# Weight conversion of the second MLP group spread over ten head slots instead of eight, its scale and split two slots later

## The chip, the core and the metric

One NeuronCore of a Trainium2 chip runs the whole program. The metric is the device time of one execution in microseconds (us); lower is better. Engine names are those of the profile: PE (matrix products), PEld (loading of PE's weights), DVE (vector), ACT (activation), POOL (GpSimd) and SP (its queue issues most loads and stores).

## What is computed

Eight batches of eight attention heads, with 576 positions of 64 numbers each, a mask by blocks of 64, softmax, and then an MLP over all 4608 tokens with d_model 512 and d_ff 2048. Cut to what matters:

```python
scores = where(block_i >= block_j, q @ k.T / 8, -1e9)          # per batch and head
attn   = softmax(scores) @ v                                    # (8, 8, 576, 64)
x      = attn.transpose(0, 2, 1, 3).reshape(4608, 512)
h      = x @ w_in                                               # (4608, 2048)
sp     = maximum(h, 0) + log1p(exp(-abs(h)))
out    = (h * erf(sp)) @ w_out                                  # (4608, 512)
```

The MLP weights arrive as 64-bit floats. The kernel splits every operand of the MLP into a high and a low 16-bit part, so that each product is three 16-bit matmuls.

## The kernel before, in words

**MLP tiling.** d_ff is cut into 16 blocks f of 128 columns, each with two halves s (w_in and w_out). The blocks form two groups: group 0 is f = 0 to 7, group 1 is f = 8 to 15. Tokens are cut into 18 tiles of 256. One piece of work is a tile with a group; it has four units of two blocks each. A unit (`moe_unit`, line 181) has 4 up steps of 6 matmuls each (line 193, h = w_in . x) followed by one gate (`gate`, line 152: ACT lines 161 to 164 and 168, DVE lines 165 to 167, POOL line 169), and 8 down steps with 12 matmuls together (line 202, o += gate . w_out). The last unit of a piece has two stores more, and in group 1 one step that loads what group 0 has stored. Group 0 of a tile stores partial sums to DRAM, group 1 adds them.

**Weights.** A half goes through three stages. `load_raw` (line 111) brings its 0.5 MB from DRAM by the SP queue (line 115, two buffers). `to_f32` (line 118, "conversion") makes 32-bit floats from the 64-bit ones: ACT lines 122 and 128, DVE lines 123, 124 and 125. When a whole group is converted, `scale_group` (line 565) finds its scale (`scale_w`, line 130: a DVE sum, a small matmul, some small DVE operations; then `scale_bg` for the batches known). Then `split_w` (line 143) makes the 16-bit parts of one block: two ACT instructions (line 148) and two DVE instructions (line 149).

**Order of the work.** The order is written out by hand in the loop over head slots n = 0 to 66. In slot n the program emits: the load of head n + 3 (lines 400 to 408), the row maxima of head n + 2 (PE line 432, DVE line 435), the probabilities of head n (PE lines 478 and 479, six pairs a slot, and ACT line 483), every second slot the product with v (line 527), and every fourth the normalisation of four heads, whose result goes to DRAM as x and is read back by `load_x` (line 225, SP queue) when a batch is complete. `merge` spreads the lists of steps evenly over the slot. The instructions go to the engines by this order as a priority: one whose inputs are there early can be placed ahead of its entry. Each engine and each queue then takes its own instructions in order.

Four tables place the rest. `TOF` says how many halves are converted in a slot, `SCALE_AT` in which slot a group's scale is made, `SPLIT` how many blocks are split in a slot. `RATE` says how often `moe1` (line 271) is called: 12 times a slot before slot 20, 28 times from slot 20 on. Each call emits one MLP step, if there is one. A unit is taken from the queue only when its blocks have been split:

```python
if jobs and len(done) >= 2 * jobs[0][2] + 2:      # in moe1: both blocks of the unit are split
    ...
if len(downs) > lag[-1] or not jobs and downs:    # the down part of an earlier unit beside it
    lists.append((downs.pop(0), 0, 1))
```

`next_job` (line 255) lets a tile into the queue when its batch is ready: tiles 0 and 1 from slot 10, tiles 2 and 3 from slot 18, tiles 4 and 5 from slot 26. Group 1 of a tile enters only after group 1 has been scaled. What the slots don't emit is emitted after slot 66 by a loop that calls `moe1` until nothing is left.

By the tables of before, group 1 is converted in slots 11 to 18 (two halves each), scaled in slot 20 and split in slots 20 to 23 (two blocks each). From slot 12 to the end of slot 66, 4 calls of `moe1` find nothing to emit; all 4 are in slot 23. After slot 66 there remain 117 up steps and 257 down steps.

Of the kernel before, what the change touches and what calls it, by code (L numbers as in the profile page):

```python
# [32 lines left out]
def tile_attention_moe(ctx: ExitStack, tc: tile.TileContext, qk, v, w, maskrows, selws, out):  # L33
# [264 lines left out]
    with tc.tile_pool(name="apool", bufs=2) as apool, tc.tile_pool(name="spool", bufs=1) as spool, \  # L298
# [266 lines left out]
        def scale_group(g):  # L565
            scale_w(g, bank)
            scaled[g] = True
            for b in known:
                scale_bg(b, g)
# [81 lines left out]
        def late(kind, steps):  # L651

            def run(f):
                tc.cur_priority += PRIO.get(kind, 0)
                f()
                tc.cur_priority -= PRIO.get(kind, 0)
            return [lambda f=f: run(f) for f in steps]
# [1 line left out]
        PRIO = {}  # L659
        WARM = 10  # L660
        LQ = 0.1
        TOF = {0: 1, 1: 1, 2: 2, 3: 2, 4: 2, 5: 2, 6: 2, 7: 2, 8: 2} | {n: 2 for n in range(11, 19)}
        SCALE_AT = {9: 0, 20: 1}
        SPLIT = {9: 2, 10: 3, 11: 3, 20: 2, 21: 2, 22: 2, 23: 2}
        def conv():
            fs = HALVES[len(conved)]
            conved.append(fs)
            if len(raws) < len(conved):
                next_raw()
            to_f32(*fs, raws[fs])  # L670
            if len(raws) == len(conved):
                next_raw()
# [11 lines left out]
        for n in range(N + 3):  # L684
# [38 lines left out]
            ready = ready_at.get(n, ready)  # L723
            for _ in range(TOF.get(n, 0)):
                lists.append((late("conv", [conv]), 0, 1))
            if n == 2:
                lists.append(([selects], 0.5, 0.6))
            if n in SCALE_AT:
                lists.append(([lambda n=n: scale_group(SCALE_AT[n])], 0, 0.1))
            if n in SPLIT:  # L730
                lists.append((late("conv", [split_next] * SPLIT[n]), 0.1, 1))
            if n < 2:
# [52 lines left out]
```

## Time and profile before

| what | value |
|---|---|
| median of 3 runs | 1236.84 us (1234.63 to 1239.13) |
| profiled execution | 1233.12 us, of which its span is 1231.3 us |
| mean granted PE clock | 0.968 of full |
| PE busy | 1149.8 us (93%) |
| DVE busy | 824.7 us (67%) |
| ACT busy | 863.3 us (70%) |
| POOL busy | 478.7 us (39%) |
| HBM | 118.15 MB read, 28.31 MB written |

The span runs from the first to the last instruction of the program. Busy shares are means over stages that differ: slots 0 to 9 are attention and weights alone, slots 11 to 66 have both attention and MLP, and the end is MLP alone. Matmuls are pipelined and their ends are modelled, so a busy PE is not yet a PE at its peak. A slot isn't marked in the trace; it is found by the six pairs of matmuls of line 478 that each head has.

### The profile page before, as it was taken

To read this page: it belongs to the slowest core of one execution; us is meant where nothing else is said; L and a number is where in the kernel's file an instruction comes from. 1 tells how busy PE (TensorE), PEld (TensorE's weight loads), DVE (VectorE), ACT (ScalarE), POOL (GpSimd) and SP (SyncE) were. 2 spreads that over 40 slices of the span, in tenths; PEclk is the share of its full clock that TensorE was granted. 3 is DMA by queue.
4 is the path that set the end of the run, shared out by engine and by line. 5 is a ranking of instruction groups with operands and counts; after the bars stand their busy time and mean duration, and the time that the engine had idled before them with its cause. 6 is when DMAs were issued, how large, how long until landed. Compare 5 with 4: busy or idle time off the path is not lost.

```text
span 1231.3 us, 23115 instructions
## 1 busy us (share of the span) xinstructions
PE 1149.8 (93%) x8874; PEld 796.0 (65%) x8874; DVE 824.7 (67%) x1559; ACT 863.3 (70%) x1675; POOL 478.7 (39%) x459
## 2 busy tenths in 40 slices
PE   6867899899999999999999999999989999999997
PEld 3545666566666667767666676776766766666663
DVE  5877887797577767677667666666667644455555
ACT  4665777577677776777777676777767776766664
POOL 7454545535444544445354444435444322100000
PEclk9876899989999999999999999999999999999999
DMA  8676667735545455453554455444544221221202
GB/s 231 171 211 161 166 186 219 179 91 122 120 133 138 110 129 124 129 136 102 124 137 95 114 125 121 115 124 116 120 114 108 57 67 57 72 69 52 65 23 85
DMA packets 94091, 148.19 MB, mean 120 GB/s; under 512 B 7610, under 2 KB 44794, under 8 KB 93982
## 3 DMA queue, kind: packets, MB, share of 16 engines
q1 hardware_dynamic: 69696, 93.34, 24.9%
q0 software_dynamic: 23616, 53.15, 20.3%
q8 instruction: 70, 1.15, 0.4%
q10 hardware_dynamic: 670, 0.23, 0.1%
q14 instruction: 39, 0.32, 0.1%
HBM read 118.15 MB, written 28.31 MB: 119 GB/s over the span
## 4 chain that ended last, share of the span: by engine, by line
PE 34%; DVE 26%; ACT 25%; DMA 7%; issue 6%; POOL 2%; ACTq 0%; DVEq 0%; SPq 0%; POOLq 0%
PE m_h L193 11%; PE o L202 10%; DVE m_r L165 6%; DVE m_r L166 5%; DVE m_r L167 5%; PE u L527 4%; ACT m_r L162 4%; ACT m_r L161 4%; ACT m_r L164 4%; ACT m_r L163 4%; ACT m_gh L168 3%; DVE mx L435 3%; PE s L432 2%; PE t L478 2%; DMA qk<-qk 2%
## 5 line engine op out<-in xcount | busy, mean ns | idle before, releaser
L193 PE MATMUL m_h<-xh,w 128*128 128x256 f16 x2304 | 473.7, 275 | 13.1 <-DVE m_r L167 12.1
L193 PEld LDWEIGHTS <-w 128*128 128x128 f16 x3456 | 327.3, 99 | 147.0 <-issue 18.1
L202 PE MATMUL o<-w,m_gh 128*128 128x512 f16 x1152 | 332.9, 382 | 4.7 <-ACT m_gh L168 3.8
L193 PE MATMUL m_h<-xl,w 128*128 128x256 f16 x1152 | 316.3, 275 | 0.0
L169 POOL TENSOR_TENSOR m_gl<-m_r,m_gh 128x512 f16<-128x512 f32 x114 | 136.1, 1193 | 267.7 <-ACT m_gh L168 234.7
L435 DVE TENSOR_REDUCE mx<-s 64x1 f32<-64x288 f32 (+4 forms) x384 | 173.9, 469 | 93.5 <-PE s L432 92.9
L165 DVE SCALAR_TENSOR_TENSOR m_r<-m_r,m_r 128x512 f32<-128x512 f32 x144 | 116.2, 807 | 166.4 <-ACT m_r L164 161.6
L168 ACT CAST m_gh<-m_r 128x512 f16<-128x512 f32 x144 | 88.9, 617 | 173.3 <-DVE m_r L167 171.5
L202 PE MATMUL o<-w,m_gl 128*128 128x512 f16 x576 | 203.7, 384 | 0.0
L483 ACT ACTIVATE p<-t 128x288 f32<-128x288 f32 (+4 forms) x384 | 143.8, 383 | 68.4 <-PE t L479 60.4
L478 PE MATMUL t<-qk 69*128 69x288 f32 (+4 forms) x384 | 167.8, 438 | 13.1 <-DVE mx L435 6.1
L432 PE MATMUL s<-qk 68*64 68x288 f32 (+3 forms) x384 | 148.5, 421 | 24.6 <-DMA qk<-qk 18.6
L408 POOL TENSOR_TENSOR qk<-st,qk 64x576 fp32r<-64x576 f32 x64 | 94.9, 1484 | 128.8 <-DMA qk<-qk 121.0
L161 ACT ACTIVATE m_r<-m_h,c,bs 128x512 f32<-128x512 f32 (+3 forms) x192 | 123.9, 665 | 28.9 <-PE m_h L193 27.4
L202 PEld LDWEIGHTS <-m_gh 128*128 128x128 f16 x1152 | 100.4, 98 | 60.9 <-issue 6.9
L495 DVE TENSOR_TENSOR p<-p,p 128x832 f16<-128x832 f32 x80 | 81.6, 1020 | 62.6 <-ACT p L494 62.5
L479 PE MATMUL t<-qk 128*128 128x288 f32 (+4 forms) x384 | 120.7, 316 | 0.0
L166 DVE SCALAR_TENSOR_TENSOR m_r<-m_r 128x512 f32<-128x512 f32 x144 | 116.7, 810 | 3.2
L405 POOL TENSOR_TENSOR qk<-st,qk 64x576 fp32r<-64x576 f32 x64 | 98.5, 1539 | 29.6 <-ACT qk L415 13.0
L163 ACT ACTIVATE m_r<-m_r,c 128x512 f32<-128x512 f32 x144 | 103.7, 720 | 2.7 <-ACT m_r L162 0.6
L164 ACT ACTIVATE m_r<-m_r,c 128x512 f32<-128x512 f32 x144 | 103.6, 719 | 2.2 <-ACT m_r L163 0.3
L162 ACT ACTIVATE m_r<-m_r,c 128x512 f32<-128x512 f32 x144 | 103.7, 720 | 2.0
(113 smaller groups left out, 1459.9 us busy)
## 6 DMA issues: line engine op xcount, KB each, us to landing
qk<-qk POOLq DMA_DIRECT2D x52, 432.0 KB, 4.7
st<-qk SPq DMA_DIRECT2D x64, 288.0 KB
qk<-qk POOLq DMA_DIRECT2D x64, 288.0 KB, 5.0
raw<-w SPq DMA_DIRECT2D x32, 512.0 KB
v<-v SPq DMA_DIRECT2D x16, 640.0 KB
x_d<-xs POOLq DMA_DIRECT2D x32, 288.0 KB, 3.3
xh<-x_d SPq DMA_DIRECT2D x36, 256.0 KB
xl<-x_d SPq DMA_DIRECT2D x36, 256.0 KB
```

The costliest lines, as they stand in the source:

```text
L161: nc.scalar.activation(r0s[:, :, lo:hi], h[:, :, lo:hi], AF.Tanh, bias=const(p1), scale=bss[b][g][:, 0:1])
L162: nc.scalar.activation(r1, r0, AF.Square, bias=const(b1), scale=a1)
L163: nc.scalar.activation(r0, r1, AF.Square, bias=const(b2), scale=a2)
L164: nc.scalar.activation(r0, r0, AF.Square, bias=const(b3), scale=a3)
L165: nc.vector.scalar_tensor_tensor(out=r0, in0=r0, scalar=c4, in1=r1, op0=ALU.add, op1=ALU.mult)
L166: nc.vector.scalar_tensor_tensor(out=r0, in0=r0, scalar=c5, in1=r0, op0=ALU.add, op1=ALU.mult)
L193: nc.tensor.matmul(h[:, k, :], lhsT=wf[:, a, sl], rhs=x[:, cc, :], start=cc == 0 and i == 0, stop=cc == NCC - 1 and i == 2)
L202: nc.tensor.matmul(o[c], lhsT=a[:, sl], rhs=wf[:, b_, :], start=u == u0 and k == 0 and not lo and b_ == 2, stop=u == u1 - 1 and k == nu - ...
L432: nc.tensor.matmul(dst[:r, :w_], lhsT=qh[:K, i * P : i * P + r], rhs=kh[:K, k0 : k0 + w_], start=True, stop=True)
L435: nc.vector.tensor_reduce(out=mx[:r, col : col + 1], in_=src, axis=AX.X, op=ALU.max, negate=True)
L478: nc.tensor.matmul(s[:kk, :w_], lhsT=kh[:K, ks], rhs=qh[:K, q0 : q0 + w_], start=True, stop=False)
L483: nc.scalar.activation(p32s[part][:kk, c : c + w_ - skip], s[:kk, skip:w_], AF.Exp, scale=SCALE)
```

## The change

It edits three of the tables. Group 1's halves are converted one a slot in slots 11 to 14 and two a slot in slots 15 to 20. Its scale goes from slot 20 to slot 22, and its blocks are split in slots 22 to 25 instead of 20 to 23, two a slot as before. Group 0's entries (slots 0 to 11) stay. No instruction is added or taken away.

```diff
-        TOF = {0: 1, 1: 1, 2: 2, 3: 2, 4: 2, 5: 2, 6: 2, 7: 2, 8: 2} | {n: 2 for n in range(11, 19)}
-        SCALE_AT = {9: 0, 20: 1}
-        SPLIT = {9: 2, 10: 3, 11: 3, 20: 2, 21: 2, 22: 2, 23: 2}
+        TOF = {0: 1, 1: 1, 2: 2, 3: 2, 4: 2, 5: 2, 6: 2, 7: 2, 8: 2} | {n: 1 for n in range(11, 15)} | {n: 2 for n in range(15, 21)}
+        SCALE_AT = {9: 0, 22: 1}
+        SPLIT = {9: 2, 10: 3, 11: 3, 22: 2, 23: 2, 24: 2, 25: 2}
```

## Rows read from the trace of the kernel before

**Rows 1.** The page, parts 1: span; busy time, share, instructions of each engine.
```profile
span 1231.3 us, 23115 instructions
PE 1149.8 (93%) x8874; PEld 796.0 (65%) x8874; DVE 824.7 (67%) x1559; ACT 863.3 (70%) x1675; POOL 478.7 (39%) x459
```

**Rows 2.** Windows, line 478 alone: stretch, its length, PE busy (instructions), PEld, clock, DMA.
```profile
130.80:192.10 61.30, 10.17 (x24) 4.40 (x24) 0.92 0.64 170
...
293.20:362.40 69.20, 10.97 (x24) 4.37 (x25) 1.00 0.50 127
362.40:1005.10 642.70, 100.38 (x223) 40.51 (x223) 1.00 0.46 115
```

**Rows 3.** Windows: stretch, length, busy PE, PEld, DVE, ACT, POOL, clock, DMA share, GB/s.
```profile
130.80:192.10 61.30, 54.72 (x402) 37.93 (x402) 54.50 (x102) 45.00 (x101) 28.75 (x26) 0.92 0.64 170
192.10:236.60 44.50, 41.28 (x307) 26.12 (x306) 37.08 (x77) 30.54 (x77) 23.98 (x23) 1.00 0.74 197
236.60:254.60 18.00, 16.01 (x101) 11.96 (x99) 10.28 (x22) 9.91 (x22) 7.35 (x8) 0.81 0.77 184
254.60:293.20 38.60, 35.92 (x274) 24.75 (x274) 33.96 (x69) 33.36 (x65) 17.23 (x14) 1.00 0.33 86
293.20:326.40 33.20, 33.20 (x255) 23.04 (x254) 18.40 (x35) 21.79 (x43) 15.84 (x16) 1.00 0.49 120
326.40:362.40 36.00, 35.19 (x270) 24.18 (x269) 24.31 (x43) 23.63 (x47) 14.46 (x13) 1.00 0.51 133
293.20:362.40 69.20, 68.39 (x523) 47.22 (x522) 42.71 (x78) 45.42 (x89) 30.30 (x29) 1.00 0.50 127
362.40:1005.10 642.70, 621.91 (x5208) 444.19 (x5206) 437.25 (x819) 475.12 (x910) 286.53 (x261) 1.00 0.46 115
1075.00:1200.00 125.00, 125.00 (x865) 84.50 (x864) 66.55 (x97) 82.45 (x127) 0.00 (x0) 1.00 0.16 51
```

**Rows 4.** Windows, line 193 alone (24 matmuls are one unit), at the end.
```profile
1075.00:1200.00 125.00, 78.58 (x576) 56.35 (x576) 1.00 0.16 51
```

**Rows 5.** Groups of DVE, 130.8 to 236.6 us: count | busy us, mean ns | idle before.
```profile
L124 DVE SCALAR_TENSOR_TENSOR w<-a,w 128x512 int32<-128x512 int32 x16 | 16.8, 1048 | 2.7 <-ACT a L122 2.6
L125 DVE SCALAR_TENSOR_TENSOR w<-a,w 128x512 int32<-128x512 int32 x16 | 15.9, 995 | 0.1
L123 DVE TENSOR_SCALAR w<-raw 128x512 int32<-128x512 int32 x14 | 9.2, 677 | 2.8 <-DMA raw<-w 2.8
```

**Rows 6.** Timeline of DVE, 166 to 174 us: start, us, instruction.
```profile
167.47 0.68 DVE L124 SCALAR_TENSOR_TENSOR w<-a,w 128x512 int32<-128x512 int32 x1
...
168.17 1.90 DVE L124 SCALAR_TENSOR_TENSOR w<-a,w 128x512 int32<-128x512 int32 x1
```

**Rows 7.** Timeline of POOL in the same stretch.
```profile
168.09 1.42 POOL L408 TENSOR_TENSOR qk<-st,qk 64x576 fp32r<-64x576 f32 x1 [4.49 <-DMA qk<-qk]
```

**Rows 8.** Groups of DVE, 254.6 to 293.2 us.
```profile
L149 DVE SCALAR_TENSOR_TENSOR w<-w,wsb,w 128x512 f16<-128x512 f32 x16 | 12.5, 799 | 1.2 <-ACT w L148 1.2
...
L563 DVE TENSOR_TENSOR bs<-bs,wsb 128x1 f32<-128x1 f32 x3 | 1.7, 560 | 0.0
L561 DVE SCALAR_TENSOR_TENSOR bs<-bi,wsb 128x1 f32<-128x1 f32 x3 | 1.6, 521 | 0.0
```

**Rows 9.** Groups of ACT, 254.6 to 293.2 us.
```profile
L148 ACT ACTIVATE w<-w,wsb 128x512 f16<-128x512 f32 x16 | 11.4, 718 | 2.5 <-DVE w L149 2.5
```

**Rows 10.** Groups of DVE, 293.2 to 362.4 us: the gate's three instructions.
```profile
L166 DVE SCALAR_TENSOR_TENSOR m_r<-m_r 128x512 f32<-128x512 f32 x9 | 8.5, 945 | 0.2
L165 DVE SCALAR_TENSOR_TENSOR m_r<-m_r,m_r 128x512 f32<-128x512 f32 x9 | 8.0, 894 | 11.7 <-ACT m_r L164 11.7
L167 DVE SCALAR_TENSOR_TENSOR m_r<-m_r,m_h 128x512 f32<-128x512 f32 x9 | 6.1, 678 | 0.1
```

**Rows 11.** Timeline of SP's queue, 200 to 262 us: loads of weights and x.
```profile
215.21 1.79 SPq L115 DMA_DIRECT2D raw<-w  x2
220.99 0.33 SPq L401 DMA_DIRECT2D st<-qk  x1
234.72 0.38 SPq L225 DMA_DIRECT2D xh<-x_d  x1
```

## The prediction

> **What bounds the kernel now.** I read the page's busy shares first: PE 93%, DVE 67%, ACT 70% [rows 1]. That is a mean over stages, so next come the windows, cut at slot borders. Line 478 runs six times a slot, so 24 of them in 130.8 to 192.1 us are slots 11 to 14, the same count in 293.2 to 362.4 us is slots 22 to 25, and 223 in the long stretch are 37 slots [rows 2]. In between lie slots 15 to 18 (192.1 to 236.6), slot 19 (to 254.6) and slots 20 and 21 (to 293.2). What the reader should see in the windows [rows 3]: three regimes. In slots 11 to 14 DVE is busy 54.5 of 61.3 us (0.89), in slots 20 and 21 34.0 of 38.6 us (0.88); there DVE is the bound, with PE waiting in short gaps. From slot 22 to 62 DVE falls to two thirds and PE is full; a slot lasts 642.7 / 37 = 17.4 us. After the last head PE is busy all the time, and nothing is hidden there: every step put there costs its full price.
>
> So the question is whether the time taken off DVE's crowded slots is more than what the later start of group 1 pushes into the end.
>
> **The steps pushed to the end (cost).** With the scale in slot 22, the queue in slot 22 holds the last unit of tile 3 in group 0 and then group 1 units, each of which waits for two splits. Splits come two a slot, so only one unit of group 1 starts in each of slots 22 to 25. One unit with the down part of an earlier one is 12 steps, and a slot has 28 calls. Going through the calls one by one, 14, 16, 16 and 14 of them find nothing in slots 22 to 25, 60 together, where before 4 did. The other 56 steps are emitted after slot 66: 17 up steps, 36 down steps and 3 stores and loads. What one costs there: 576 matmuls of line 193 at 24 a unit are 24 units in 125 us, or 5.2 us a unit [rows 4]. 17 up steps are 4.25 units, 36 down steps 4.5; 4.4 units x 5.2 = **+22.8 us**. It has no cover, since PE is full there [rows 3], and its ends are close (+22 to +24).
>
> **Slots 22 to 25 (gain).** They lose the same 4.4 units and take 69.2 us now [rows 3]. If PE stayed the bound they would take 69.2 - 22.8 = 46.4 us. But they now receive the scale and the splits, and fewer gates. The trace shows where splits run: all 16 DVE split instructions lie in slots 20 and 21 [rows 8], though two of the four slots of their table are later, so they are placed ahead as soon as they can run; I take it that all 16 lie in slots 22 to 25 after. DVE there: 42.7 us now [rows 3]; less 18 up steps, which are 4.5 gates of 0.95 + 0.89 + 0.68 = 2.5 us [rows 10], 11.3 us; plus 12.5 us of splits [rows 8]; plus about 5 us of scale and small operations, of which the two largest groups are 1.7 and 1.6 us [rows 8]. Sum 49 us. That is more than PE's 46.4, so DVE is the bound, and at its share in the two crowded stretches, 0.885, the four slots take 49 / 0.885 = 55 us: **-14 us**. ACT gets 11.4 us more [rows 9] and loses the gates' own activations; it stays below. Ends: -20 (DVE full, 49 us) and -11 (all splits fall into slots 22 and 23, which then do not get shorter at all, and only slots 24 and 25 give their 30 empty calls, 30 / 12 x 5.2 = 13, less 2).
>
> **Slots 11 to 14 (gain).** Four conversions leave. One is 1.05 + 1.00 + 0.68 = 2.7 us of DVE by the means of this stretch [rows 5]; rounded with the two L123 that ran before it, 2.6, so 10.5 us. DVE falls from 54.5 to 44 us. At 0.885 busy the stretch would take 49.7 us, 11.6 less. The nearest stretch with less work in it, slots 15 to 18, reaches only 37.1 / 44.5 = 0.83 [rows 3], and 44 / 0.83 = 53: **-8 us**, which I take, since PE has about as much to do as DVE then. Ends: -12 and -2; the small end, because the waits in slot 11 for x and for the splits of group 0 stay.
>
> Part of that DVE time is not the conversion's own: the same instruction took 0.68 us alone and 1.90 us when it began 0.08 us after a POOL instruction [rows 6, 7]. Without such overlap a conversion is about 3 x 0.68 = 2.0 us, and 4 of them 8.2. The Trainium skill ("SBUF — State Buffer", section "Who interferes with whom") says that a DVE instruction with two SBUF inputs and a GpSimd instruction lock each other out of a shared port for a whole instruction; the pair in the rows agrees. By that rule the block would pass to the next DVE instruction of that kind, and the term would be 8 x 8.2 / 10.5, about -6 rather than -8.
>
> **Slots 19 to 21.** Slot 19 gets two conversions, 5.3 us of DVE into 7.7 us of idle time [rows 3]. Their raw loads come late: x loads wait at the head of SP's queue until 234.7 us, and the raw loads for slots 19 and 20 stand behind them, where the last raw loads now go out at 215 us [rows 11]. Conversions mixed into the gates then delay PE, which waits for them in this slot: **+2 us** (0 to +5.3). Slots 20 and 21 lose the scale and the splits, 17.5 us, and get two conversions: 34.0 - 17.5 + 5.3 = 21.8 us of DVE in 38.6. They become PE bound like the slots behind, 2 x 17.4 = 34.7: at most -3.9, I take **-3 us** (0 to -4).
>
> **Elsewhere.** POOL and the x, qk and v loads keep their slots; half a MB less is loaded in each of slots 11 to 14 and one MB more in slots 19 and 20, where DMA is at 0.77 and 0.33 [rows 3]. Counted at nothing beyond the +2.
>
> **Sum:** 22.8 - 14 - 8 + 2 - 3 = -0.2 us, no change. The profiled execution took 1233.1 us, 3.7 below the median of the runs shown (1236.84); the forecast for the median is 1236.6. A difference of under 0.3%, 3.7 us, can't be told from none.
>
> **Rivals.**
> Relief wins (faster). DVE was the true limit in slots 11 to 14, the full -12 comes; and in slots 22 to 25 the freed PE time is filled by later heads and units that are placed ahead, as the splits are now, so that they come near -18. Sum 22.8 - 18 - 12 + 2 - 3 = -8, or 1229. For it: DVE at 0.89 in slots 11 to 14. Against: in slots 15 to 18 DVE was busy 0.83 only [rows 3], and nothing placed ahead filled PE there.
> DVE pile-up with a falling clock (slower). All 16 splits run in slots 22 and 23, where DVE then has 18.4 - 5 + 12.5 + 5 = 31 us and the two slots stay at 33 to 35 us: -11 instead of -14. PE waits between its bursts, and the clock drops as in slots 11 to 14 (0.92) or slot 19 (0.81) [rows 3]. At 0.92 a share of 0.16 of some 57 us runs at 1.2 GHz, and half of these 9 us is lost: +4.5. Sum +7.3, or 1244. It decides when DVE is over 0.9 busy in slots 22 and 23 and the granted clock there is under 0.95. The Trainium skill ("TensorE: Matmul & The Clock Gate", section "What's actually happening") says that half rate is the default and activity releases it, which speaks against a change that thins PE's work; the rows agree for slot 19, and slots 15 to 18, at clock 1.00 with 12 calls a slot, do not.
> The change does not do what it says: if the placing undid the tables, the splits would run as early as now and nothing would move; they can't run before the scale, so I give this little.
>
> **Chances.** Forecast case 0.42 (of it 0.28 within 0.3%, 0.07 beyond on either side), relief wins 0.28, pile-up 0.30 (0.02 of it within 0.3%). That makes faster 0.35, same 0.30, slower 0.35. The terms' ends, taken together, reach from -13 (22.8 - 20 - 12 + 0 - 4) to +15, which is unlikely all at once; the range is 1225 to 1250 and holds both rivals. The forecast case by itself lies in 1232 to 1241.
>
> **What would show it.** At the end, from the last head on, some 23 us more; slots 22 to 25 near 55 us with DVE near 0.88 and the splits inside; slots 11 to 14 near 53 us; slots 20 and 21 near 35 us. If slots 22 to 25 take over 60 us, or slots 11 to 14 stay at 60, it gets slower; if the first are near 50, faster. A raw load that lands after its conversion's turn in slot 19 would show as DVE waiting for it.

## The result and the profile after

The changed kernel takes 1245.34 us (median of 15 runs), the kernel before 1234.63 beside it: a ratio of 1.0087, interval 1.0068 to 1.0107, so 8 to 13 us slower. The forecast was no change. The page of after, part 1:

```profile
span 1249.7 us, 23108 instructions
PE 1153.9 (92%) x8874; PEld 795.5 (64%) x8874; DVE 825.3 (66%) x1563; ACT 865.5 (69%) x1675; POOL 474.4 (38%) x455
```

Busy times are those of before to within 5 us [rows 1]: the work is the same, the waiting is not. The windows of after, cut at the same heads as [rows 3] (columns as there): slots 11 to 14, 15 to 18, 19, 20 and 21, 22 and 23, 24 and 25, 26 to 62.

```profile
133.40:189.30 55.90, 53.06 (x405) 37.20 (x403) 42.54 (x90) 40.12 (x88) 27.87 (x26) 0.94 0.56 146
189.30:240.70 51.40, 44.27 (x308) 28.21 (x307) 37.89 (x78) 31.21 (x77) 23.05 (x23) 0.93 0.76 193
240.70:257.50 16.80, 15.45 (x97) 11.54 (x97) 7.09 (x14) 8.94 (x18) 7.31 (x6) 0.82 0.73 188
257.50:296.70 39.20, 36.65 (x279) 24.91 (x276) 26.80 (x55) 29.73 (x64) 16.64 (x17) 1.00 0.49 125
296.70:321.90 25.20, 23.98 (x185) 15.88 (x185) 22.37 (x58) 20.77 (x42) 14.06 (x14) 1.00 0.54 115
321.90:352.10 30.20, 26.40 (x191) 17.23 (x189) 24.32 (x39) 20.14 (x40) 12.17 (x11) 0.94 0.54 127
...
352.10:997.70 645.60, 619.91 (x5199) 442.09 (x5196) 439.99 (x817) 474.00 (x906) 287.47 (x261) 1.00 0.45 116
```

DVE's load left slots 11 to 14 as meant (54.5 to 42.5 us), but the stretch got only 5 us shorter, and slots 15 to 18, with the same conversions as before, longer. Slots 22 to 25 fell from 69.2 to 55.4 us. All 16 DVE splits of group 1 ran in them, 10 in slots 22 and 23; their row for 296.7 to 352.1 us:

```profile
L149 DVE SCALAR_TENSOR_TENSOR w<-w,wsb,w 128x512 f16<-128x512 f32 x16 | 13.8, 887 | 1.1 <-ACT w L148 1.0
```

Then the end, from the last head on, which [rows 3] shows only in part; before first, then after:

```profile
1005.10:1231.30 226.20, 214.59 (x1497) 141.55 (x1495) 115.71 (x171) 148.00 (x233) 14.38 (x13) 0.99 0.19 62
```

```profile
997.70:1249.70 252.00, 237.95 (x1658) 157.37 (x1655) 129.52 (x192) 164.62 (x258) 15.66 (x14) 0.99 0.18 60
```

161 matmuls more, 25.8 us more. That is where the time went, against 14 us gained in slots 22 to 25.

Executions of one kernel differ by some us, so stretches are compared over all traces. The table has the length of each in us, cut at the first probability matmul of heads 11, 15, 19, 20, 22, 26 and 63 (the experiments follow below; "empty" is the number of calls of moe1 from slot 12 on that find nothing or are left out):

| kernel | empty | 0-10 | 11-14 | 15-18 | 19 | 20-21 | 22-25 | 26-62 | end |
|---|---|---|---|---|---|---|---|---|---|
| before | 4 | 130.8 | 61.3 | 44.5 | 17.9 | 38.7 | 69.2 | 642.6 | 226.3 |
| before_again | 4 | 128.5 | 60.3 | 44.5 | 15.6 | 38.7 | 69.8 | 643.3 | 228.0 |
| after | 60 | 133.4 | 55.8 | 51.4 | 16.8 | 39.2 | 55.4 | 645.6 | 252.1 |
| after_again | 60 | 127.9 | 55.3 | 46.3 | 14.3 | 41.6 | 54.7 | 646.4 | 252.0 |
| delay_alone | 60 | 132.1 | 61.4 | 44.1 | 15.8 | 35.9 | 53.7 | 648.7 | 252.0 |
| spread_no_delay | 4 | 127.2 | 55.8 | 46.6 | 25.8 | 34.0 | 70.6 | 644.9 | 226.7 |
| four_left_out | 4 | 131.2 | 55.9 | 46.7 | 15.6 | 38.7 | 71.3 | 642.2 | 229.5 |
| splits_at_once | 0 | 129.8 | 56.3 | 49.5 | 15.9 | 39.2 | 74.9 | 635.8 | 226.4 |
| raw_in_free_slot | 60 | 131.0 | 57.0 | 48.0 | 17.0 | 39.0 | 52.8 | 644.4 | 253.6 |
| rate_from_18 | 0 | 131.7 | 61.3 | 43.0 | 32.9 | 42.1 | 70.0 | 637.8 | 210.9 |
| before_splits_once | 0 | 130.1 | 60.2 | 44.5 | 16.7 | 38.3 | 71.9 | 635.2 | 224.7 |
| delay_splits_once | 0 | 131.1 | 61.3 | 44.1 | 16.1 | 35.9 | 75.3 | 632.7 | 227.3 |
| half_rate_30_33 | 60 | 131.6 | 61.4 | 46.0 | 17.1 | 38.6 | 69.6 | 628.6 | 253.5 |
| spread21_once_rate19 | 0 | 131.8 | 55.7 | 46.8 | 25.6 | 38.9 | 71.4 | 634.7 | 218.3 |
| once_less4 | 4 | 131.8 | 60.6 | 45.9 | 14.7 | 39.2 | 72.0 | 643.5 | 228.0 |
| before_less8 | 12 | 132.1 | 59.6 | 46.1 | 17.8 | 38.8 | 70.4 | 630.9 | 232.5 |

Slots 0 to 10 have the same plan in all kernels and still range over 127 to 133 us: that much is chance. Most later stretches repeat within 2 to 4 us where two kernels have the same plan. Slots 15 to 18 of the spread do not: its plan for slots 11 to 18 stands in after, after_again, splits_at_once, raw_in_free_slot and spread21_once_rate19, and they take 46.3 to 51.4 us, 48.4 in the mean, where the kernels with the plan of before take 44.1 to 46.1. The 51.4 is of the slowest run of after.

### The profile page after: what moved, and what is told of

It reads as the page before. It is cut to its first block, busy times and chain, and to the rows that moved or that the text cites. A ratio compares the mean times of both kernels' runs of the same rounds, so it can differ in the third digit from the quotient of the medians.

```text
span 1249.7 us, 23108 instructions
## 1 busy us (share of the span) xinstructions
PE 1153.9 (92%) x8874; PEld 795.5 (64%) x8874; DVE 825.3 (66%) x1563; ACT 865.5 (69%) x1675; POOL 474.4 (38%) x455
## 4 chain that ended last, share of the span: by engine, by line
PE 45%; DVE 21%; ACT 19%; DMA 8%; issue 4%; POOL 2%; ACTq 0%; SPq 0%; DVEq 0%; POOLq 0%
PE m_h L193 15%; PE o L202 15%; DVE m_r L166 5%; PE u L527 5%; DVE m_r L165 5%; DVE m_r L167 3%; ACT m_r L161 3%; ACT m_r L162 3%; ACT m_r L164 3%; ACT m_r L163 3%; DMA v<-v 3%; PE s L432 3%; PE t L478 2%; PE t L479 2%; DMA qk<-qk 2%
## 5 line engine op out<-in xcount | busy, mean ns | idle before, releaser
L166 DVE SCALAR_TENSOR_TENSOR m_r<-m_r 128x512 f32<-128x512 f32 x144 | 122.3, 849 | 2.9
```

Of the source, the lines that this page charges most:

```text
L166: nc.vector.scalar_tensor_tensor(out=r0, in0=r0, scalar=c5, in1=r0, op0=ALU.add, op1=ALU.mult)
```

## The experiments

Two theories stood at first: the delay of scale and splits makes the loss (theory 1), or the spread conversions do (theory 2). Four kernels went together.

**delay_alone**, against the kernel before:

```diff
-        SCALE_AT = {9: 0, 20: 1}
-        SPLIT = {9: 2, 10: 3, 11: 3, 20: 2, 21: 2, 22: 2, 23: 2}
+        SCALE_AT = {9: 0, 22: 1}
+        SPLIT = {9: 2, 10: 3, 11: 3, 22: 2, 23: 2, 24: 2, 25: 2}
```

> The delay alone: conversions as before (two a slot in slots 11 to 18), scale in slot 22, splits in slots 22 to 25. The forecast's terms for the two late parts were +22.8 us at the end, -14 in slots 22 to 25 and about -3 in slots 20 and 21, so about +6 us against the kernel before; slots 11 to 19 should last as before. Theory 1 (the delay makes the slower result, and the relief of the conversions is worth little): +8 to +13 us, as much as the whole change. Theory 2 (the spread conversions cost time of their own, by raw weights that land late): +3 to +7 us here, and the rest of the change's loss appears only where the conversions are spread.

Measured: 1.0074 (1.0046 to 1.0101), +9 us. Theory 1 holds. Its windows for slots 20 and 21, and for 22 to 25:

```profile
253.40:289.30 35.90, 35.90 (x279) 25.00 (x276) 19.25 (x37) 24.68 (x50) 15.12 (x14) 1.00 0.39 107
...
289.30:343.00 53.70, 48.77 (x372) 32.36 (x372) 45.88 (x96) 41.15 (x83) 26.29 (x24) 1.00 0.57 127
```

Slots 20 and 21, free of scale and splits, are PE bound and 2.8 us shorter, as the forecast had it for them. Slots 22 to 25 are as short as in after, at a granted clock of 1.00.

**spread_no_delay**, against the kernel before:

```diff
-        TOF = ... | {n: 2 for n in range(11, 19)}
+        TOF = ... | {n: 1 for n in range(11, 15)} | {15: 2, 16: 2, 17: 2, 18: 3, 19: 3}
```

> The spread alone: one half a slot in slots 11 to 14, two in 15 to 17, three in 18 and 19; scale and splits as before, so the number of MLP steps left for the end is that of before. Theory 1: slots 11 to 14 some 5 us shorter, slots 15 to 19 as much longer, total within 3 us of the kernel before. Theory 2: slots 15 to 19 over 8 us longer, total +3 to +8 us. The forecast's own reading (DVE is the bound in slots 11 to 14 and has room in slot 19): -8 + 3 = -5 us.

Measured: 1.0028 (0.9997 to 1.0058). The 5 us of slots 11 to 14 are there, and slot 19 alone takes 25.8 us instead of 16 to 18; slots 20 and 21 get 5 us back. Slots 15 to 19 are 10 to 12 us longer, as theory 2 had it, and the total lies on the border of the two theories; its interval holds no change. The spread does not pay.

**four_left_out**, against the kernel before (the zeros are set at the start):

```diff
-        TOF = ... | {n: 2 for n in range(11, 19)}
+        TOF = ... | {n: 1 for n in range(11, 15)} | {n: 2 for n in range(15, 19)}
...
-        HALVES = [(f, i) for f in range(NF) for i in range(2)]
+        HALVES = [(f, i) for f in range(NF - 2) for i in range(2)]
...
+            for t in (raw_t(NF - 2), raw_t(NF - 1), wss[1]):
+                nc.gpsimd.memset(t, 0.0)
```

> Four of the 32 conversions of weights are left out, with their loads (the last two blocks are zero instead): one half a slot in slots 11 to 14, two in slots 15 to 18, scale and splits as before. That is the relief without its price. The forecast's term for it was -8 us (ends -12 and -2), all of it in slots 11 to 14. Theory 1 (something else than DVE sets the pace there): 0 to -3 us over slots 11 to 18, what slots 11 to 14 gain being given back in slots 15 to 18. Theory 2: -6 to -10 us, kept to the end.

Measured: 0.9975 (0.9949 to 1.0000), -3 us. Slots 11 to 14 and 15 to 18:

```profile
131.20:187.10 55.90, 52.63 (x403) 37.08 (x402) 43.29 (x87) 39.90 (x89) 28.61 (x27) 0.94 0.59 146
187.10:233.80 46.70, 42.38 (x307) 27.16 (x306) 36.63 (x77) 30.52 (x77) 24.57 (x23) 0.96 0.74 195
```

With 11 us of DVE taken away (54.5 to 43.3 [rows 3]) and put nowhere, slots 11 to 14 gain 5 us, and slots 15 to 18 give 2 of them back. The whole relief is worth 3 us at the end. PE is busy 52.6 of the 55.9 us of slots 11 to 14 (0.94), as in after (53.1): with DVE relieved, PE is busy for nearly all of the stretch.

**after_again** is the changed kernel once more.

> The changed kernel once more, for a second trace and beside the three others on the same chip: +8 to +13 us against the kernel before. Slots 15 to 18, 7 us longer in the first trace, show by this trace whether that belongs to the kernel (over 4 us longer again) or to that one execution; the end should again be 23 to 26 us longer and slots 22 to 25 about 14 us shorter.

Measured: 1.0101 (1.0065 to 1.0137). Slots 15 to 18 are 46.3 us here, 2 over before: 5 of the 7 us of the first trace belonged to that execution. With the three other traces of this plan the mean is some 3 to 4 us over before.

The second four ask whether the empty calls are the loss, and what late raw weights cost.

**splits_at_once**, against the changed kernel:

```diff
-        SPLIT = {9: 2, 10: 3, 11: 3, 22: 2, 23: 2, 24: 2, 25: 2}
+        SPLIT = {9: 2, 10: 3, 11: 3, 22: 8}
```

> The changed kernel with all eight splits emitted in slot 22 instead of two in each of slots 22 to 25: conversions and scale stay as changed, but group 1's units are no longer held back, no call of moe1 comes up empty, and the steps left after slot 66 are 371 up and down steps against 374 before and 427 changed. Theory 1 (the loss is the 56 empty calls: 26 us more at the end for 14 us less in slots 22 to 25): the end falls back to 225 us, slots 22 to 25 come back to some 68 to 72 us, and the total is 8 to 12 us below the changed kernel, within 3 us of the kernel before. Rival (the splits themselves and the late conversions cost the time): total stays 5 us or more above the kernel before.

Measured: 0.9954 (0.9934 to 0.9973), 5 us faster than before and some 16 below the changed kernel, more than theory 1 asked for. Slots 22 to 25, 26 to 62 and the end:

```profile
290.60:365.50 74.90, 71.32 (x539) 48.67 (x538) 56.74 (x112) 57.11 (x108) 33.95 (x31) 1.00 0.50 122
365.50:1001.30 635.80, 618.97 (x5202) 442.68 (x5200) 431.37 (x816) 474.52 (x906) 280.68 (x259) 1.00 0.45 116
1001.30:1227.70 226.40, 212.92 (x1488) 141.01 (x1485) 115.47 (x170) 148.48 (x234) 15.61 (x14) 0.99 0.19 61
```

The end is back at 226 us and slots 22 to 25 at 75. But slots 26 to 62 fell by 7 us against before, which neither theory had.

**raw_in_free_slot**, against the changed kernel. In after_again DVE waits for a raw half in slot 20; its timeline, and SP's queue in the same stretch:

```profile
248.94 0.40 DVE L123 TENSOR_SCALAR w<-raw 128x512 int32<-128x512 int32 x1
252.73 0.43 DVE L123 TENSOR_SCALAR w<-raw 128x512 int32<-128x512 int32 x1 [3.39 <-DMA raw<-w]
```

```profile
231.25 12.37 SPq L401 DMA_DIRECT2D st<-qk  x2
243.79 2.10 SPq L115 DMA_DIRECT2D raw<-w  x2
```

```diff
-        raw = pool.tile([P, 2 * DM], I32, tag="raw", name=f"raw{f}_{s}", bufs=2)
+        raw = pool.tile([P, 2 * DM], I32, tag="raw", name=f"raw{f}_{s}", bufs=2) if (f, s) != (NF - 1, 0) else i32(raw_t(GA - 1))
```

> The changed kernel, but the raw half before the last has a place of its own (a weight slot that is free from slot 11 to the first split), so that the last two raw loads no longer wait for the two raw buffers. In both traces of the changed kernel DVE waits in slot 20 for a raw half that was asked for late (3.4 us in the second). Theory (late raw weights are what keeps slots 20 and 21 at 39 to 42 us, where the kernel with the delay alone has 36): that wait goes, slots 20 and 21 fall to 36 to 38 us, total 2 to 4 us below the changed kernel. Rival (the wait is cover for other work): within 1.5 us of the changed kernel.

Measured: 1.0095 (1.0075 to 1.0114), no gain. DVE's timeline in this run, line 123 in slot 18 (up to 236.0 us) and in slot 20:

```profile
234.72 0.43 DVE L123 TENSOR_SCALAR w<-raw 128x512 int32<-128x512 int32 x1 [3.46 <-DMA raw<-w]
...
257.39 0.41 DVE L123 TENSOR_SCALAR w<-raw 128x512 int32<-128x512 int32 x1
```

The wait in slot 18 stands in both traces of the changed kernel too. The one in slot 20 is gone, and slots 20 and 21 stay at 39.0 us: the rival holds, that wait was cover for other work. The pairs show that the conversions cost slots 20 and 21 some 3 us: 35.9 us in both delayed kernels without them, 39.0 to 41.6 in the four traces of delayed kernels that have them. What in the conversions costs it stays open.

**rate_from_18**, against the kernel before:

```diff
-        SPLIT = {9: 2, 10: 3, 11: 3, 20: 2, 21: 2, 22: 2, 23: 2}
+        SPLIT = {9: 2, 10: 3, 11: 3, 20: 4, 21: 4}
...
-            lists.append((... RATE[0 if n < 10 else 1 if n < 20 else 2]), 0, 1))
+            lists.append((... RATE[0 if n < 10 else 1 if n < 18 else 2]), 0, 1))
```

> The opposite of the change, on the kernel before: 28 calls of moe1 a slot from slot 18 on instead of slot 20, with the splits four a slot in slots 20 and 21; no empty call, 339 up and down steps after slot 66 instead of 374. By the price seen at the end (25.7 us for 53 steps, 0.48 us each) the end is 16 to 17 us shorter; slots 18 and 19 take 32 steps more. Theory 1 (a step costs its full price at the end and about half of it in slots where PE isn't full: 14.5 us for 56 steps, 0.26 each): +8 us in slots 18 and 19, total -8 us against the kernel before. Rival (slots 18 and 19 wait for x and for the gates, and steps put there cost as much as at the end): total within 2 us.

Measured: 0.9973 (0.9956 to 0.9991). Slot 19 and the end:

```profile
236.00:268.80 32.80, 28.47 (x194) 20.44 (x193) 18.51 (x36) 22.43 (x43) 14.38 (x13) 0.95 0.53 127
1018.70:1229.60 210.90, 200.29 (x1399) 132.59 (x1396) 106.03 (x157) 139.22 (x220) 15.55 (x14) 0.99 0.18 59
```

The end is 16 us shorter, slot 19 some 16 longer: the 32 steps that slots 18 and 19 got cost there about what they save at the end, as the rival had it. PE waits there for gates (3.1 us) and hardly for x (0.2). The total of -3 us lies between the two forecasts; the gain comes from slots 26 to 62 again (637.8).

**before_again** is the kernel before once more.

> The kernel before once more, for a second trace: total within 2 us of the runs of the kernel before. It shows how far the stretches differ between two executions of one kernel: slots 0 to 10 (127 to 133 us in the other traces, the plan being the same), slots 11 to 14 (61), 20 and 21 (39), 22 to 25 (69), 26 to 62 (642 here, 645 to 649 with the delay) and the end (226).

Measured: 0.9997 (0.9977 to 1.0017); its stretches are in the table.

The third four split the gain of splits_at_once, and price emptied calls where nothing else happens.

**before_splits_once**, against the kernel before:

```diff
-        SPLIT = {9: 2, 10: 3, 11: 3, 20: 2, 21: 2, 22: 2, 23: 2}
+        SPLIT = {9: 2, 10: 3, 11: 3, 20: 8}
```

> The kernel before with all eight splits emitted in slot 20 instead of two in each of slots 20 to 23: no empty call where before had 4. It asks where the 5 us come from by which the changed kernel with its splits in one slot beats the kernel before. Theory A (the spread conversions are worth some 5 us once no call is empty): this kernel is at -1 to -2 us (four steps less at the end), the gain stays away. Theory B (it is the order of the MLP steps without a gap, the stretch of slots 26 to 62 being 636 to 638 us in both kernels without an empty call and 643 to 649 in all others): -4 to -7 us, slots 26 to 62 at 635 to 639.

Measured: 0.9921 (0.9898 to 0.9943), 10 us faster than before. Theory B holds: slots 26 to 62 are at 635.

```profile
361.80:997.00 635.20, 620.13 (x5202) 443.40 (x5200) 431.20 (x816) 474.34 (x906) 280.84 (x259) 1.00 0.45 116
```

**delay_splits_once**, against the kernel before:

```diff
-        SCALE_AT = {9: 0, 20: 1}
-        SPLIT = {9: 2, 10: 3, 11: 3, 20: 2, 21: 2, 22: 2, 23: 2}
+        SCALE_AT = {9: 0, 22: 1}
+        SPLIT = {9: 2, 10: 3, 11: 3, 22: 8}
```

> Conversions as before, scale in slot 22 and all eight splits in slot 22: the late scale alone, with no call empty. Theory 1 (lateness costs nothing in itself, only the calls it empties do): -6 to +2 us against the kernel before, some 10 us below the kernel with the delay and two splits a slot. Theory A expects 3 to 5 us more than the spread kernel with its splits at once (about 0 against before), theory B the same as that one (-5).

Measured: 0.9928 (0.9901 to 0.9954), the same as with the scale in slot 20. A late scale costs nothing in itself. With the spread on top (splits_at_once) it is 0.9954: three pairs (this one, spread_no_delay against before, after against delay_alone) put the spread alone at +0.1 to +0.3%, none of them clear of noise by itself.

**half_rate_30_33**, against the kernel before:

```diff
-            lists.append((... RATE[0 if n < 10 else 1 if n < 20 else 2]), 0, 1))
+            lists.append((... (14 if 30 <= n < 34 else RATE[0 if n < 10 else 1 if n < 20 else 2])), 0, 1))
```

> The kernel before with 14 instead of 28 calls of moe1 in slots 30 to 33: 56 steps fewer there, 56 more after slot 66, and no scale, split or conversion near. It prices the emptied calls apart from what the change puts beside them. The end should again be 25 to 26 us longer. Theory 1 (in slots 22 to 25 DVE, busy with scale and splits, kept the slots from shrinking by more than 14 us): here DVE has room, slots 30 to 33 shrink by 19 to 23 us and the total is +3 to +6 us. Rival (PE alone sets what a slot gives back, attention being slow by itself at this rate): they shrink by 12 to 15 us and the total is +9 to +13 us.

Measured: 1.0080 (1.0053 to 1.0107), +10 us, as the whole change. Slots 30 to 33 of before, then of this run, and its end:

```profile
431.00:498.60 67.60, 66.63 (x562) 47.54 (x559) 45.27 (x84) 49.87 (x96) 31.59 (x28) 1.00 0.49 120
```

```profile
431.40:484.00 52.60, 48.49 (x412) 34.47 (x410) 37.27 (x72) 36.03 (x74) 26.84 (x24) 0.97 0.53 128
...
993.00:1246.50 253.50, 238.17 (x1658) 157.37 (x1655) 129.59 (x192) 164.67 (x258) 15.67 (x14) 0.99 0.18 59
```

DVE is busy 37.3 of 52.6 us (0.71) with no split near, and the four slots are still 15 us shorter only. So it does not take scale and splits on DVE to keep a thinned slot from giving all of its steps back.

**spread21_once_rate19**, against the changed kernel:

```diff
-        SCALE_AT = {9: 0, 22: 1}
-        SPLIT = {9: 2, 10: 3, 11: 3, 22: 2, 23: 2, 24: 2, 25: 2}
+        SCALE_AT = {9: 0, 21: 1}
+        SPLIT = {9: 2, 10: 3, 11: 3, 21: 8}
...
-            lists.append((... RATE[0 if n < 10 else 1 if n < 20 else 2]), 0, 1))
+            lists.append((... RATE[0 if n < 10 else 1 if n < 19 else 2]), 0, 1))
```

> A version meant to beat both: conversions spread as changed, scale and all eight splits in slot 21, and 28 calls of moe1 a slot from slot 19 on. No call is empty; 355 up and down steps after slot 66 instead of 374 before and 427 changed. By 0.48 us a step the end is 8 to 9 us shorter than before, slots 19 to 22 take 4 to 8 us of that back, and the spread with no empty call was worth 5 us: -5 to -9 us against the kernel before. If steps put into slot 19 cost their full price there, as the 28 calls in slots 18 and 19 did (16 us more there, 15 less at the end), -5 us.

Measured: 0.9920 (0.9897 to 0.9942), no better than the one-line before_splits_once. Both beat both kernels.

The last two ask why slots 26 to 62 change.

**once_less4** is before_splits_once with 4 calls left out in slot 26; **before_less8** is the kernel before with 8:

```diff
-            lists.append((... RATE[0 if n < 10 else 1 if n < 20 else 2]), 0, 1))
+            lists.append((... (24 if n == 26 else RATE[0 if n < 10 else 1 if n < 20 else 2])), 0, 1))
...
-            lists.append((... RATE[0 if n < 10 else 1 if n < 20 else 2]), 0, 1))
+            lists.append((... (20 if n == 26 else RATE[0 if n < 10 else 1 if n < 20 else 2])), 0, 1))
```

> The kernel before with all splits emitted in slot 20 (which was 10 us faster than before), and 4 calls of moe1 left out in slot 26. From slot 26 on the MLP steps then stand against the heads as in the kernel before, which has 4 empty calls in slot 23, with no split near. Theory P (what is worth 7 to 8 us in slots 26 to 62 is only how the MLP steps lie against the heads): slots 26 to 62 go back to 641 to 645 us, and the total is within 3 us of the kernel before. Rival (it comes from the splits being done early): slots 26 to 62 stay at 635 to 637 and the total is -6 to -10 us.

> The kernel before with 8 calls of moe1 left out in slot 26, so that with the 4 empty ones of slot 23 one whole round of 12 steps (a unit's up steps with the down steps of an earlier one) is missing, and the steps lie against the heads as they do without any empty call, one unit later. Theory P, if only the place within a round counts: slots 26 to 62 at 633 to 638 us, end 4 us longer than before, total -2 to -6 us. If the identity of the unit counts too (the changed kernel misses five whole rounds and has 646 us there), slots 26 to 62 stay at 641 to 646 and the total is +2 to +6 us.

Measured: 0.9982 (0.9965 to 0.9999) and 0.9923 (0.9894 to 0.9951). Slots 26 to 62 of the first, then of the second:

```profile
364.20:1007.60 643.40, 621.16 (x5191) 443.17 (x5190) 435.74 (x817) 473.01 (x906) 282.32 (x259) 0.99 0.45 114
```

```profile
364.80:995.60 630.80, 616.15 (x5182) 441.13 (x5181) 429.95 (x815) 473.43 (x906) 286.07 (x260) 1.00 0.47 118
```

Theory P holds: four calls missing bring the stretch from 635 to 643 us with the splits left early, and twelve missing (4 in slot 23, 8 in slot 26) bring it to 631 with the splits left late. Of those 12 us some 2 to 4 are only the 8 steps that left the stretch, an estimate from 0.26 to 0.45 us a step as priced below. It is the place of the MLP steps against the heads, not how early the splits run. Where part of it shows: slots 40 to 45 take 109.4 us in before and 103.3 in before_splits_once, and the waits of PE for a gate there are, before first:

```profile
PE m_h L193 <- DVE m_r L167: 3.5, 3, 2.1
```

```profile
PE m_h L193 <- DVE m_r L167: 0.7, 2, 0.5
```

Up steps stand waiting for the gate that frees their accumulator. That is 2.8 of the 6.1 us; PE is also busy 2.2 us longer there (104.1 against 101.9), at a granted clock of 0.98 against 1.00.

## Why the prediction was wrong, point by point

The sum was -0.2 us, the difference of the medians is +10.7. By halves, the forecast had the delay at +5.8 (22.8 - 14 - 3) and the spread at -6 (-8 + 2); the runs show +9 for the delay and +1 to +3 for the spread. So most of the miss is the relief of slots 11 to 14, which was counted as kept. Against the mean of two traces each, which lie 14.2 us apart rather than 10.7:

- **The end (+22.8).** Right in kind, sized too low: +24.9. The steps were counted right, the matmuls are 23 us of PE's busy time; the rest of the 25.8 in the first pair is waiting of PE in the last 31 us.
- **Slots 22 to 25 (-14).** The number held (-14.4), the reason fell, so that was luck. The forecast made DVE the bound there by the scale and splits, at 49 us and a share of 0.885. All 16 splits did run there, as it said, and DVE was busy 46.7 of 55.4 us (0.84). But half_rate_30_33 shrinks four slots by the same 15 us with DVE at 0.71 and no split. In both places four slots with half the MLP steps give back about 15 of the 24 us that 56 steps are at 5.2 us for 12. What keeps the other 9 was not taken apart.
- **Slots 11 to 14 (-8). This is the first step that failed.** Measured -5.2, and four_left_out shows only -3 left at the end even when the work is put nowhere. A DVE busy at 0.89 was read as the bound. With 0.76 the stretch was 5 us shorter and PE was busy 53 of its 56 us: PE had been busy 54.7 of 61.3 before [rows 3], the same 0.89, so PE had few idle us to give back. The Trainium skill's rule of the shared port ("SBUF — State Buffer", "Who interferes with whom") made the term -6, nearer for the stretch, but not for its reason. By that reading four conversions take 8.2 us off DVE; DVE's busy time fell by 10.8 to 12.0 us in after, after_again and four_left_out, more than the plain 10.5. No run took POOL's work away, so the rule itself stays untested here.
- **Slots 15 to 18 (0).** +2 in one trace and +7 in the other: most of the relief is given back. Slots 11 to 18 together are 0.9 us shorter in these pairs, against the 8 forecast. What makes slots 15 to 18 longer was not taken apart.
- **Slots 19 to 21 (+2 and -3). The second step that failed.** Slot 19 was 1 us shorter, slots 20 and 21 were 1.7 longer. That they drop to 36 us without scale and splits was right (delay_alone); that conversions hide there was not, the three that ran in them cost 3 us and more. DVE was waiting for raw weights, as the text named, in slot 20 (2.0 and 3.4 us) rather than 19, but raw_in_free_slot, without that wait, is no faster.
- **Elsewhere (0). The third.** Slots 26 to 62 took 3 us more. They were counted at nothing. A shift of the MLP steps against the heads can be worth 8 us there (once_less4), but the change shifts them by two whole slots, as the last paragraph of this section says, and the 3 us stay open.
- **The rivals.** The slower one gave 1244 and the time was 1245, but by another way: clock and pile-up are not it. 10 of the 16 splits ran in slots 22 and 23, not all, and these took 25.2 us at a clock of 1.00, not 33 to 35. In delay_alone the clock of slots 22 to 25 is 1.00, and they are as short as in after, where it is 0.94 in the second half. So the rule of the clock gate that was weighed there ("TensorE: Matmul & The Clock Gate", "What's actually happening", in the Trainium skill) does not carry this loss. The faster rival's premise, that later work fills the freed PE time, did not come about: PE is busy 50.4 of 55.4 us in slots 22 to 25.

What remains as the cause, shown by runs: of +10.7 us, +9 is the delay (delay_alone), and that is the 56 empty calls: without them the same delay costs nothing (delay_splits_once at 0.9928, before_splits_once at 0.9921), and 56 calls left out elsewhere cost the same (half_rate_30_33, +10). The empty calls come from the split table, two blocks a slot, standing behind a queue that has run out of group 0 work. The spread costs the other 1 to 3 us, which no pair shows clear of noise.

Open in part: the kernels with 60 empty calls by slot 25 have 644 to 649 us in slots 26 to 62, not 635. The text put on record for before_less8 took 60 calls for five whole rounds. They are not: a round with the last unit of a tile has 14 or 15 steps. Counted call by call through the tables, the 56 steps by which the change shifts the MLP are two slots of 28 calls, and from slot 26 on the changed kernel emits in slot n what the kernel before emits in slot n - 2 (slots 37 to 42 apart, where the order of the pieces differs). So its steps lie inside the slots as in before, and not as in the kernels at 635. Why it then takes 1 to 6 us more than the 643 of before, no run took apart.

## What to carry to other kernels

When a schedule is written out by slots, first count the calls that find nothing to do: work that slips out of a stretch where it is partly hidden into an end where nothing is hidden costs the difference of the two prices, here 0.45 us a step against 0.26 (24.9 and 14.4 us for 56 steps). A busy share of 0.89 is not yet a bound; the test is to leave the work out, and here 11 us less of it were worth 3. And before reading a small gain as the effect of an edit, shift the schedule by a few steps alone: here 4 steps are worth 8 us of one stretch by themselves.

## What the runs showed that was not expected

One line, all splits emitted in the slot of the scale, makes the kernel before 10 us faster (0.9921), though the splits already ran that early on the engines. The emitted order of the splits holds back only the MLP steps that the program emits after them; 4 empty calls in slot 23 shifted all later steps against the heads. And slots 0 to 10, the same in every kernel, took 127 to 133 us from one execution to the next.
